# Another order of issue, and other engines for some copies, in the second feed-forward of an attention kernel

## The chip, the core and the metric

The kernel runs on one core of a Trainium2 chip. TensorE (PE) multiplies matrices into PSUM, VectorE (DVE) and ScalarE (ACT) do the work between matmuls, and SyncE (SP) issues the DMA transfers. Each engine works through its own list of instructions in order and waits on semaphores for the others. PEld is PE's weight load, which the profile shows apart. The metric is the device time of the program in microseconds.

## The reference

Windowed attention with global tokens gives 2176 rows of 512 numbers for the feed-forwards, which follow one another:

```python
def reference(**kwargs):
    ...
    attn_out = _attn_ref(**attn_kwargs)
    B, H, S, D = attn_out.shape
    x = np.ascontiguousarray(attn_out.transpose(0, 2, 1, 3)).reshape(B * S, H * D)
    x = _moe_ref(x=x, **moe_kwargs)      # h = x @ w_in;  (h * tanh(softplus(h))) @ w_out
    return _moe2_ref(x=x, **moe2_kwargs)
...
def _moe2_ref(x, w_in, w_out) -> np.ndarray:
    h = x @ w_in
    g = h * np.cos(h)
    return (g @ w_out).astype(np.float32)
```

All is float32; x is 2176 x 512, w_in 512 x 2048, w_out 2048 x 512. The attention and the first feed-forward are the same in both kernels.

## The kernel before

**Products in three parts.** A float32 matmul is made of three passes of a narrower type: each operand is split into a high and a low part, and low x high, high x high and high x low are added in PSUM. The high part is a cast (`gh`), the low part the difference (`gl`).

**The second feed-forward** is the function `second` (L952). It works in 24 steps s = 0 to 23: two halves p of the hidden units, three pairs of token blocks b (two of 384 tokens each, the last pair of 320 each), four groups of units j. Steps 0 to 11 are p = 0, steps 12 to 23 p = 1; steps 8 to 11 and 20 to 23 are the 320-wide pair. One step has these parts, which a list names by a letter, a number and the step:

- `P0` to `P6` (L1019): the first matrix product. A 2 x 2 block product is made of seven products in place of eight; the combined blocks of x are the operands 0 to 6. Each is six matmuls into one of two PSUM banks that they take in turns.
- `E0` to `E7` (L1041): the sums of those seven into the hidden values `hs`. `E0` is a copy of the product into `u`, the others are additions on DVE. A bank is free for the next product only when its sum or sums are done.
- `f0` to `f6`, `g0` to `g6` (in the last step `a`, `b`, `c`, `d`): h cos h for the two halves of the units. ACT does the first pair of operations (L831, L832) and a later pair (L841, L842), DVE L835, L838, L845; number 5 is the cast into `gh`, number 6 the difference `gl` on DVE (L851).
- `U0` to `U5`, `V0` to `V5` (L1050): units of the second product, three matmuls of 512 columns each, on accumulators 0 to 5 (one for each 128 tokens), U for the first half of the hidden units of a step and V for the second. They add up over the four steps j of a pair.
- `Z0` to `Z5`: an accumulator is emptied after step j = 3: copied into `part` (p = 0) or added to it on DVE and stored to the output (p = 1, L1068).
- `X`, `Y`: the weights of U or V are used up, and SP loads those of the next half into their place (L430, `w<-scr`). `A`, `I`, `L`: the operands of the next pair are formed, cast and stored to memory (L919, L345 or L347, L932, L940); after each product of a step j = 3 SP loads the operand of the next pair (L950 for `xo`, L947 for `xq`).
- `R`, `S`: what is left of the first feed-forward, in step 0.

**Tiles of PSUM.** Accumulators 0 and 1 are single banks (`acc_...`). Accumulators 2 and 3 are the halves of one tile, 4 and 5 of another (both named `h_...`). The program's dependencies go by tile: a unit on one half waits for a copy that reads the other half, and a copy of one half waits for a unit on the other.

**What sets the order.** A list written out by hand, the string `ORDER2` (L68), has some 1,079 entries such as `P0:11` or `Z5:7d`. It is run from its start to its end (L1080), and each entry issues its instructions on the engines that they belong to, DMAs included; so it sets the order on every engine at once. A last letter chooses the engine of a copy or cast (`move`, L341): d is DVE (L345), a is ACT (L347).

```python
        for step in ORDER2.split():
            name, _, n = step.partition(":")
            at2["at"] = n[-1:]
            steps[name](int(n.rstrip("ad")))
```

Which half of which tile an accumulator is, and which bank a product takes, stands in these lines:

```python
                single = [late["ps"].tile([P, 512], F32, tag="acc", name="acc", bufs=4) for _ in range(4)]
                acc.extend(single[2:4] + [t[:, c] for t in (ps2, ps) for c in range(2)] + single[0:2])
...
            i = (s + o) % 2
...
            return singles()[6 + i][:, 0:n_of(s)]
```

Of the kernel before, what the change touches and what calls it, by code (L numbers as in the profile page):

```python
# [65 lines left out]
"""  # L66

ORDER2 = """  # L68
    I6:0d L5:0 I0:1a P0:0 P1:0 E0:0d L6:0 P2:0 R:0 E1:0 I4:1a E2:0 L4:1 P3:0 P4:0 A5:1 E3:0 L0:1 E4:0 A3:1 f0:0
# [4 lines left out]
    P0:3 f0:2 P1:3 f1:2 V5:0 g5:1a E0:3a E1:3 U0:1 A6:1 P2:3 U4:1 f2:2 g6:1 f3:2 P3:3 I6:1d g0:2 U1:1 V1:1 E2:3
    f4:2 P4:3 L6:1 E3:3 E4:3 g1:2 U2:1 g2:2 U3:1 L4:2 U5:1 P5:3 P6:3 V3:1 f5:2a E6:3 g3:2 V0:1 f0:3 E7:3 A5:2 E5:3
    V2:1 P0:4 P1:4 g4:2 g5:2a E0:4a f6:2 V5:1 f1:3 A3:2 U2:2 E1:4 f2:3 P2:4 P3:4 E2:4 U5:2 P4:4 V4:1 U4:2 U0:2 f3:3
    g0:3 I0:2a g6:2 g1:3 E3:4 E4:4 g2:3 U1:2 f4:3 f0:4 g3:3 U3:2 f5:3a P6:4 P5:4 E6:4 E5:4 V5:2 L0:2 E7:4 V0:2 P0:5
    V4:2 E0:5a g4:3 f6:3 P1:5 g5:3a V3:2 f1:4 E1:5 I1:2d P2:5 P3:5 V1:2 U4:3 f2:4 V2:2 E2:5 I3:2a f3:4 E3:5 P5:5
    P4:5 g6:3 L1:2 L3:2 U0:3 V0:3 f4:4 g0:4 I5:2a U2:3 g1:4 U3:3 g2:4 A2:2 V4:3 V2:3 E4:5 P6:5 g3:4 E5:5 E6:5 E7:5
    g4:4 P0:6 P1:6 U1:3 Z4:3d f0:5 E0:6d U5:3 V1:3 f5:4a E1:6 f6:4 f1:5 A6:2 I2:2d Z0:3a f2:5 g5:4a P2:6 P3:6 E2:6  # L80
    f3:5 E3:6 V3:3 Z1:3a U0:4 V5:3 U4:4 P5:6 L5:2 g6:4 P4:6 f4:5 g0:5 V0:4 Z3:3d g1:5 U1:4 U3:4 E6:6 Z5:3a E4:6
    V3:4 E5:6 g2:5 f5:5a I6:2a L6:2 Z2:3a U5:4 P6:6 f0:6 f6:5 V1:4 E7:6 P0:7 U2:4 f1:6 P1:7 E0:7d g3:5 g4:5 L2:2
    P2:7 E1:7 V2:4 f2:6 V4:4 g5:5d E2:7 g0:6 U3:5 f3:6 P3:7 g6:5 P4:7 E3:7 E4:7 g1:6 f4:6 V5:4 g2:6 f5:6d f6:6 U1:5
    U4:5 f0:7 P5:7 g3:6 E6:7 P6:7 f1:7 U0:5 U2:5 E5:7 f2:7 V1:5 f3:7 E7:7 g4:6 V2:5 V0:5 P0:8 U5:5 P1:8 g5:6d E0:8a
    P2:8 f4:7 U0:6 V4:5 E1:8 E2:8 g6:6 P4:8 P3:8 g0:7 g1:7 V3:5 U4:6 E3:8 E4:8 P5:8 V5:5 U1:6 U2:6 g2:7 U5:6 E5:8
    E6:8 P6:8 P0:9 f0:8 g3:7 E7:8 f5:7d f6:7 U3:6 V5:6 f1:8 P1:9 E0:9d f2:8 g4:7 V1:6 V4:6 P2:9 g0:8 U1:7 E1:9
    g5:7d V3:6 g6:7 U4:7 g1:8 E2:9 f3:8 P3:9 P4:9 f4:8 U3:7 E3:9 P5:9 g2:8 V0:6 V2:6 U0:7 E5:9 E4:9 P6:9 f5:8d V3:7
    g3:8 f0:9 E6:9 E7:9 g4:8 U5:7 P0:10 P1:10 U2:7 f6:8 Z3:7a V1:7 E0:10d V2:7 P2:10 g5:8a E1:10 f1:9 f2:9 Z1:7d
# [5 lines left out]
    f4:11 g3:11 P6:12 P5:12 U0:10 E6:12 E5:12 f5:11d f0:12 U3:10 f6:11 E7:12 Z5:7d Y:8 P0:13 g4:11 V4:10 U2:10
    V2:10 f1:12 f2:12 E0:13a P1:13 g0:12 P2:13 E1:13 g5:11d P3:13 E2:13 g6:11 V1:10 P4:13 g1:12 V3:10 U1:11 X:8
    E3:13 E4:13 f3:12 V0:10 P5:13 P6:13 U2:11 g2:12 f4:12 E5:13 E6:13 g3:12 E7:13 P0:14 E0:14a P1:14 g4:12 E1:14
    f5:12a V2:11 f0:13 f6:12 P2:14 P3:14 U4:11 V4:11 V1:11 Z4:11a f1:13 U3:11 U0:11 E2:14 Z1:11a V3:11 Y:9 P4:14
    Z2:11a f2:13 U4:12 E3:14 E4:14 U5:12 P5:14 f3:13 g0:13 g5:12d V0:11 U1:12 U2:12 f4:13 g6:12 P6:14 g1:13 g2:13
    V5:12 E5:14 g3:13 E6:14 P0:15 E7:14 Z3:11d Z0:11d V2:12 U3:12 P1:15 E0:15d f5:13a f0:14 U0:12 X:9 g4:13 f6:13
    V0:12 f1:14 E1:15 P2:15 E2:15 V3:12 V1:12 f2:14 P3:15 g5:13d Y:10 E3:15 U5:13 P4:15 g6:13 g0:14 P5:15 g1:14  # L100
    U0:13 U1:13 E4:15 f3:14 f4:14 E6:15 g2:14 E5:15 U3:13 P6:15 E7:15 g3:14 g4:14 P0:16 U2:13 V2:13 V4:12 f5:14a
    P1:16 E0:16d P2:16 V1:13 U4:13 E1:16 V4:13 f0:15 X:10 g5:14a P3:16 X:11 f6:14 E2:16 f1:15 f2:15 P4:16 g0:15
    E3:16 f3:15 g6:14 P5:16 U4:14 V5:13 E4:16 V3:13 g1:15 U5:14 U3:14 g2:15 f0:16 P6:16 f4:15 g3:15 E6:16 E5:16
    P0:17 V0:13 E7:16 E0:17a U0:14 P2:17 f5:15a U1:14 g4:15 P1:17 f6:15 U2:14 V1:14 f1:16 E1:17 V5:14 E2:17 f2:16
    P4:17 Y:11 P3:17 V4:14 V0:14 V3:14 E3:17 g5:15d g6:15 f3:16 f4:16 E4:17 P5:17 g0:16 V2:14 Y:20 g1:16 P6:17
    E5:17 E6:17 U3:15 V3:15 g2:16 U1:15 E7:17 U4:15 P0:18 E0:18d P1:18 g3:16 g4:16 U0:15 f5:16d E1:18 P2:18 f0:17
    P3:18 f6:16 V1:15 U5:15 V5:15 U2:15 f1:17 E2:18 f2:17 f3:17 Z1:15 V4:15 E3:18 P5:18 f4:17 P4:18 g0:17 Z4:15
    Z3:15 Y:21 V2:15 U3:16 E4:18 Z5:15 g5:16a g6:16 V0:15 E5:18 E6:18 Z2:15 P6:18 U1:16 g1:17 V1:16 U4:16 U5:16
    g2:17 f5:17d f0:18 f6:17 V4:16 P0:19 V5:16 Z0:15 g3:17 E7:18 f1:18 g4:17 U2:16 U0:16 U5:17 g5:17d f2:18 E0:19a
    V3:16 P2:19 P1:19 U3:17 E1:19 f3:18 f4:18 E2:19 V0:16 P3:19 X:20 U4:17 E3:19 g0:18 g6:17 P4:19 V2:16 g1:18  # L110
    E4:19 P5:19 U2:17 g2:18 P6:19 E6:19 U1:17 E5:19 V4:17 f5:18a V5:17 E7:19 g3:18 P0:20 g4:18 f6:18 U0:17 E0:20d
    f0:19 g5:18d P1:20 f1:19 P2:20 E1:20 V0:17 f2:19 P3:20 E2:20 V2:17 f3:19 g6:18 U4:18 E3:20 P4:20 f4:19 P5:20
    E5:20 U5:18 E4:20 E6:20 V1:17 V5:18 V3:17 g0:19 P0:21 Y:22 P6:20 U2:18 g1:19 g2:19 U0:18 E7:20 f5:19d U3:18
# [1136 lines left out]
```

## Time and profile before

| what | us |
|---|---|
| median of three runs | 885.45 (883.87 to 886.25) |
| the profiled run | 883.55 |
| its span in the trace | 881.8 |
| PE busy in the span | 860.8 (98%) |
| DVE busy | 738.2 (84%) |
| ACT busy | 483.3 (55%) |

The mean granted clock of PE is 0.997 of full speed. The second feed-forward takes the time from 508.6 us to the end. In a timeline each row is one instruction or a run of equal ones, with its start, its length, how many they are (x6), and in brackets how long the engine had been idle before and what released it. Matmuls are pipelined, so a row's length reaches into the next row: the pace of PE is read from one start to the next.

### The profile page before, as it was taken

The numbers are of one execution on the slowest core, as the hardware profiler recorded it, in microseconds if no ns is written. First come the engines' busy times: TensorE is split into PE (matmuls) and PEld (weight loads), VectorE is DVE, ScalarE is ACT, GpSimd is POOL, SyncE is SP. The second block draws the span as 40 slices with busy tenths as digits, with TensorE's granted clock in tenths as the row PEclk, the third lists the DMA queues.
The fourth block names the chain that finished last, engine by engine and source line by source line (L and its number), as shares of the span: only waits on it lengthen the run. The fifth ranks groups of instructions, "written<-read, shape, count | busy, mean of one in ns | idle before, by whom it ended". The sixth has DMA issues, their size and how long they took to land.

```text
span 881.8 us, 16128 instructions
## 1 busy us (share of the span) xinstructions
PE 860.8 (98%) x5995; PEld 790.4 (90%) x5995; DVE 738.2 (84%) x1513; ACT 483.3 (55%) x948; POOL 85.9 (10%) x137
## 2 busy tenths in 40 slices
...
GB/s 161 198 158 161 168 152 74 49 156 215 233 252 266 328 338 361 286 294 237 277 243 193 387 414 220 283 90 148 234 144 321 109 14 355 1 79 202 1 60 72
DMA packets 133886, 174.98 MB, mean 198 GB/s; under 512 B 77872, under 2 KB 100400, under 8 KB 133808
## 3 DMA queue, kind: packets, MB, share of 16 engines
...
## 4 chain that ended last, share of the span: by engine, by line
PE 76%; DMA 10%; DVE 8%; ACT 3%; issue 2%; SPq 0%; POOL 0%; DVEq 0%; ACTq 0%; POOLq 0%
PE acc L1019 17%; PE acc L1118 14%; PE h L1050 13%; PE acc L1050 7%; PE h L795 5%; PE h L797 5%; PE h L796 5%; DMA cs<-in_moe_w_out_dram 4%; DMA cs<-in_moe_w_in_dram 2%; PE s L563 2%; PE av L633 1%; DVE ca L237 1%; DMA op<-stage 1%; PE ta L606 1%; DVE x L772 1%
## 5 line engine op out<-in xcount | busy, mean ns | idle before, releaser
L1118 PE MATMUL acc<-gh,w 128*128 128x384 f32 (+1 forms) x768 | 187.9, 328 | 0.0
L1118 PEld LDWEIGHTS acc<-gh,w 128*128 128x128 f32 x768 | 136.2, 189 | 0.0
L1118 PE MATMUL acc<-gl,w 128*128 128x384 f32 (+1 forms) x384 | 126.2, 329 | 2.9 <-DVE x L868 1.9
L795 PE MATMUL h<-x,w 128*128 128x384 f32 (+1 forms) x384 | 126.1, 328 | 0.6 <-DVE x L772 0.5
L797 PE MATMUL h<-x,w 128*128 128x384 f32 (+1 forms) x384 | 125.2, 326 | 0.0
L796 PE MATMUL h<-x,w 128*128 128x384 f32 (+1 forms) x384 | 125.1, 326 | 0.0
L1050 PE MATMUL h<-w,gh 128*128 128x512 f32 x352 | 109.8, 393 | 0.0
L1019 PE MATMUL acc<-xo,w 128*128 128x384 f32 (+1 forms) x402 | 76.4, 327 | 1.6 <-DVE hs L1041 1.6
L1050 PEld LDWEIGHTS h<-w,gh 128*128 128x128 f32 x352 | 66.1, 188 | 11.8
L1118 PEld LDWEIGHTS acc<-gl,w 128*128 128x128 f32 x384 | 72.6, 189 | 4.2 <-DVE x L868 2.2
L1019 PEld LDWEIGHTS acc<-xo,w 128*128 128x128 f32 x402 | 68.0, 188 | 6.6 <-DVE hs L1041 2.8
L841 ACT ACTIVATE w<-w 128x768 f32<-128x768 f32 (+2 forms) x50 | 39.0, 780 | 63.5 <-DVE w L838 63.5
L795 PEld LDWEIGHTS h<-x,w 128*128 128x128 f32 x384 | 72.1, 188 | 1.5 <-issue 0.8
L796 PEld LDWEIGHTS h<-x,w 128*128 128x128 f32 x384 | 72.1, 188 | 0.0
L797 PEld LDWEIGHTS h<-x,w 128*128 128x128 f32 x384 | 72.1, 188 | 0.0
L1050 PE MATMUL h<-w,gl 128*128 128x512 f32 x176 | 69.2, 393 | 2.2 <-DVE part L345 1.0
L1041 DVE TENSOR_TENSOR hs<-u,acc 128x384 f32<-128x384 f32 (+1 forms) x91 | 47.4, 526 | 28.3 <-PE acc L1019 26.9
L831 ACT ACTIVATE k<-hs,magic 128x768 f32<-128x768 f32 (+2 forms) x50 | 43.5, 871 | 49.2 <-DVE w L838 43.1
L1050 PE MATMUL acc<-w,gh 128*128 128x512 f32 x192 | 59.9, 393 | 0.0
L582 ACT ACTIVATE pr<-pr,nm 128x160 f32<-128x160 f32 x128 | 53.2, 421 | 10.6 <-DVE nm L579 10.4
L835 DVE SCALAR_TENSOR_TENSOR w<-k,hs 128x768 f32<-128x768 f32 (+2 forms) x50 | 44.0, 881 | 8.2 <-ACT k L832 6.5
L822 DVE TENSOR_TENSOR gl<-w,gh 128x768 fp32r<-128x768 f32 (+1 forms) x48 | 43.5, 907 | 8.3 <-ACT gh L818 8.3
...
## 6 DMA issues: line engine op xcount, KB each, us to landing
...
xo<-op SPq DMA_DIRECT2D x10, 640.0 KB, 4.9
```

Source lines behind the costliest of these rows:

```text
L582: nc.scalar.activation(out=pr[:, i], in_=pr[:, i], func=AF.Exp, bias=nm[:, i:i + 1], scale=-1.0, accum_out=l[:, i:i + 1])
L795: nc.tensor.matmul(ps[:, c, 0:n], wh[:, k, :], xl, start=(k == 0), stop=False)
L796: nc.tensor.matmul(ps[:, c, 0:n], wh[:, k, :], xh, start=False, stop=False)
L797: nc.tensor.matmul(ps[:, c, 0:n], wl[:, k, :], xh, start=False, stop=(k == NK - 1))
L822: nc.vector.tensor_tensor(out=gl, in0=v["w"], in1=gh.bitcast(F32), op=ALU.subtract)
L831: nc.scalar.activation(out=k[:, y], in_=of("h")[:, z], func=AF.Identity, scale=INV2PI, bias=magic[:, 0:1])
L835: nc.vector.scalar_tensor_tensor(out=of("t")[:, z], in0=k[:, y], scalar=-C1, in1=of("h")[:, z], op0=ALU.mult, op1=ALU.add)
L841: nc.scalar.activation(out=of("t")[:, z], in_=of("t")[:, z], func=AF.Sin, scale=0.5)
L1019: nc.tensor.matmul(to, l[:, i + c], r, start=c == 0 and m == 0, stop=c == 1 and m == 2)
L1041: nc.vector.tensor_tensor(out=of[out](), in0=of[x](), in1=bank(s, o), op=ALU.add)
L1050: nc.tensor.matmul(singles()[a], l[:, a * P:(a + 1) * P], r, start=(j, c) == (0, 0) and m == 0, stop=(j, c) == (3, 1) and m == 2)
L1118: nc.tensor.matmul(o[:, 0:n], w[:, a * P:(a + 1) * P], r[:, c, :], start=(not goes_on and g == 0 and m == 0), stop=(not stays and g == G - ...
```

## The change

Only the string `ORDER2` is another. It holds the same entries, but stands in another order from its first line to its last, and some copies and casts change engine: of the copies Z of p = 0 twelve are on ACT and not nine, of the E0 sixteen and not fourteen, of the operand casts I thirteen and not eleven, of the casts f5 and g5 twenty-five and not twenty-four. Instructions on PE and DMA transfers are the same in number and size. As text, around the end of step 11 (before, then after):

```diff
...
-    P6:11 U4:9 g3:10 g4:10 V4:9 f4:10 V2:8 f5:10a V1:9 f0:11 E5:11 E6:11 P0:12 E7:11 V0:9 f6:10 E0:12a P1:12 P2:12
+    V0:9 f6:10 g2:10 U2:9 P5:11 V2:9 E4:11 g3:10 E5:11 U4:9 g4:10 E6:11 V4:9 P6:11 g5:10d Z5:7d f0:11 P0:12 E7:11
...
```

Three places follow as the engines see them. A row names the line, the operation, what is written, what is read and the shape; numbers behind names tell buffers apart, and are not the same in the two kernels.

**First place: the end of step 10 and P0 of step 11.** `part` is the copy Z, `u` and `hs` the sums, `h_6599` the tile of accumulators 2 and 3, `acc_6762` and `acc_6763` the two banks of the products before, `acc_6768` and `acc_6769` after. DVE before:

```order
L835 SCALAR_TENSOR_TENSOR w_7888<-k_6598,hs_7770 128x640
L838 SCALAR_TENSOR_TENSOR w_7888<-k_6598,w_7888 128x640
L345 COPY part_7815<-h_6599 128x512
L1041 TENSOR_TENSOR u_6597<-u_6597,acc_6763 128x320
L1041 TENSOR_TENSOR hs_7896<-u_6597,acc_6763 128x320
L1041 TENSOR_TENSOR hs_7896<-u_6597,acc_6762 128x320
L345 COPY part_7815<-h_6596 128x512
```

Behind the copy of `h_6599` stand three sums. PE before, with P0:11 as the sixth row:

```order
L1050 MATMUL h_6599<-w1_0_6516,gh_7781 128x512 x2
L1019 MATMUL acc_6762<-xq_6600,w0_5_6481 128x320 x3
L1019 MATMUL acc_6762<-xq_6601,w0_5_6481 128x320 x3
L1050 MATMUL h_6599<-w1_1_6518,gl_7869 128x512
L1050 MATMUL h_6599<-w1_1_6518,gh_7831 128x512 x2
L1019 MATMUL acc_6763<-xo_6128,w0_6_6551 128x320 x6
```

The product on `acc_6763` stands directly behind the unit V3:8 on `h_6599`. DVE after:

```order
L835 SCALAR_TENSOR_TENSOR w_7874<-k_6598,hs_7772 128x640
L851 TENSOR_TENSOR gl_7897<-w_7807,gh_7876 128x640
L838 SCALAR_TENSOR_TENSOR w_7874<-k_6598,w_7874 128x640
L1041 TENSOR_TENSOR hs_7900<-u_6597,acc_6769 128x320
L1041 TENSOR_TENSOR u_6597<-u_6597,acc_6769 128x320
L1041 TENSOR_TENSOR hs_7900<-u_6597,acc_6768 128x320
L835 SCALAR_TENSOR_TENSOR w_7917<-k_6598,hs_7842 128x640
L345 COPY part_7837<-acc_6770 128x512
```

The sums have no copy of `h_6599` ahead of them; those copies are on ACT. PE after, with P0:11 as the last row:

```order
L1019 MATMUL acc_6769<-xq_6591,wt_6376 128x320 x3
L1019 MATMUL acc_6769<-xq_6592,wt_6376 128x320 x3
L1019 MATMUL acc_6768<-xq_6606,w0_5_6481 128x320 x3
L1019 MATMUL acc_6768<-xq_6607,w0_5_6481 128x320 x3
L1050 MATMUL acc_6771<-w1_0_6516,gl_7805 128x512
L1050 MATMUL acc_6771<-w1_0_6516,gh_7796 128x512 x2
L1050 MATMUL h_6599<-w1_0_6516,gl_7805 128x512
L1050 MATMUL h_6599<-w1_0_6516,gh_7796 128x512 x2
L1050 MATMUL h_6599<-w1_1_6518,gl_7849 128x512
L1050 MATMUL h_6599<-w1_1_6518,gh_7811 128x512 x2
L1050 MATMUL h_6599<-w1_2_6584,gl_7897 128x512
L1050 MATMUL h_6599<-w1_2_6584,gh_7876 128x512 x2
L1019 MATMUL acc_6769<-xo_6128,w0_6_6551 128x320 x6
```

Between the product on `acc_6769` (two rows at the top, P5:10) and the next one there are now a product and four units.

**Second place: Z5:7, the copy of accumulator 5 out of the tile `h_6596`, and the next unit on that tile.** DVE before:

```order
L1041 TENSOR_TENSOR u_6597<-u_6597,acc_6763 128x384
L1041 TENSOR_TENSOR hs_8130<-u_6597,acc_6763 128x384
L345 CAST gh_8132<-w_8065 128x640
L851 TENSOR_TENSOR gl_8139<-w_8065,gh_8132 128x640
L1041 TENSOR_TENSOR hs_8130<-u_6597,acc_6762 128x384
L345 COPY part_8142<-h_6596 128x512
L845 SCALAR_TENSOR_TENSOR w_8103<-w_8103,hs_8037 128x640
```

The copy is the sixth row. PE before:

```order
L1050 MATMUL h_6599<-w1_4_6745,gh_8030 128x512 x2
L1019 MATMUL acc_6763<-xo_6128,w0_2_7696 128x384 x6
L1050 MATMUL h_6596<-w1_5_6747,gl_8085 128x512
L1050 MATMUL h_6596<-w1_5_6747,gh_8083 128x512 x2
L1050 MATMUL h_6599<-w1_4_6745,gl_8050 128x512
```

The unit V4:10 on `h_6596` (w1_5) is on the other half of that tile. DVE after:

```order
L845 SCALAR_TENSOR_TENSOR w_7984<-w_7984,hs_7900 128x640
L1041 TENSOR_TENSOR u_6597<-u_6597,acc_6768 128x320
L345 CAST gh_8048<-w_7984 128x640
L345 COPY part_8050<-h_6596 128x512
L1041 TENSOR_TENSOR hs_8028<-u_6597,acc_6769 128x320
L835 SCALAR_TENSOR_TENSOR w_8061<-k_6598,hs_7966 128x640
L345 COPY u_6597<-acc_6768 128x384
```

The copy now stands ahead of the last sum of step 11 (`hs_8028`, E7:11). PE after, from the product that this sum reads (P6:11):

```order
L1019 MATMUL acc_6769<-xq_6606,w0_7_6553 128x320 x3
L1019 MATMUL acc_6769<-xq_6607,w0_7_6553 128x320 x3
L1019 MATMUL acc_6768<-xo_6128,w0_0_7596 128x384 x6
L1050 MATMUL acc_6771<-w1_3_6586,gl_7981 128x512
L1050 MATMUL acc_6771<-w1_3_6586,gh_7979 128x512 x2
L1019 MATMUL acc_6769<-xo_6128,w0_0_7596 128x384 x6
L1019 MATMUL acc_6768<-xo_6128,wb_6369 128x384 x6
L1050 MATMUL h_6599<-w1_3_6586,gl_7981 128x512
L1050 MATMUL h_6599<-w1_3_6586,gh_7979 128x512 x2
L1019 MATMUL acc_6769<-xo_6128,w0_1_7655 128x384 x6
L1019 MATMUL acc_6768<-xo_6128,wt_6368 128x384 x6
L1019 MATMUL acc_6769<-xq_6591,wt_6368 128x384 x3
L1019 MATMUL acc_6769<-xq_6592,wt_6368 128x384 x3
L1050 MATMUL h_6596<-w1_4_6738,gl_8007 128x512
```

The next unit on `h_6596` (U4:10) is the last row; none of the rows between writes that tile.

**Third place: SP's queue while steps 12 to 15 run.** `w0_` and `w1_` are weights, `xo` the operands. Before:

```order
L430 DMA w0_7_8015<-scr31_0_6221 128x1024
L430 DMA w1_1_8144<-scr25_1_5602 128x1024
L430 DMA w1_0_8210<-scr24_1_5467 128x1024
L430 DMA w1_3_8303<-scr27_1_5810 128x1024
L950 DMA xo_6128<-op1_0_6664 128x1536
L950 DMA xo_6128<-op1_1_6810 128x1536
L430 DMA w1_2_8393<-scr26_1_5703 128x1024
L950 DMA xo_6128<-op1_2_6876 128x1536
L950 DMA xo_6128<-op1_3_6827 128x1536
```

The load of w1_2 stands behind two operand loads. After:

```order
L430 DMA w0_7_8046<-scr31_0_6221 128x1024
L430 DMA w1_2_8112<-scr26_1_5703 128x1024
L430 DMA w1_1_8171<-scr25_1_5602 128x1024
L430 DMA w1_4_8220<-scr28_1_5945 128x1024
L430 DMA w1_3_8223<-scr27_1_5810 128x1024
L430 DMA w1_5_8271<-scr29_1_6059 128x1024
L950 DMA xo_6128<-op1_0_6699 128x1536
L950 DMA xo_6128<-op1_1_6869 128x1536
L430 DMA w1_6_8379<-scr30_1_6207 128x1024
L430 DMA w1_7_8388<-scr31_1_6297 128x1024
```

Five loads of w1 stand ahead of the first operand load.

## Rows read from the trace of the kernel before

**Rows 1.** Page, span and section 1: busy us (share), instructions, by engine.

```profile
span 881.8 us, 16128 instructions
...
PE 860.8 (98%) x5995; PEld 790.4 (90%) x5995; DVE 738.2 (84%) x1513; ACT 483.3 (55%) x948; POOL 85.9 (10%) x137
```

**Rows 2.** Waits of PEld, 508 to 882: us in total, times, longest us.

```profile
PEld acc L1019 <- DVE hs L1041: 4.0, 7, 2.0
PEld h L1050 <- DVE part L345: 1.6, 2, 1.3
```

**Rows 3.** Chain that ended last: start us, us, what; pieces without a wait.

```profile
734.56 2.10 PE acc L1019 x12
...
809.86 0.88 PE acc L1019 x6
...
813.88 0.69 PE h L1050 x3
```

**Rows 4.** Timeline of PE: start us, us, engine line op out<-in xcount [idle before <-releaser].

```profile
529.97 0.39 PE L1050 MATMUL h<-w,gl 128*128 128x512 f32 x1
...
531.33 0.96 PE L1019 MATMUL acc<-xq,w 128*128 128x384 f32 x4 [0.50 <-DVE hs L1041]
...
543.98 1.31 PE L1019 MATMUL acc<-xq,w 128*128 128x384 f32 x6
...
661.84 0.39 PE L1050 MATMUL h<-w,gl 128*128 128x512 f32 x1
...
664.27 2.02 PE L1019 MATMUL acc<-xo,w 128*128 128x320 f32 x12 [1.57 <-DVE hs L1041]
...
693.31 1.23 PE L1019 MATMUL acc<-xo,w 128*128 128x384 f32 x6
695.52 0.50 PE L1050 MATMUL h<-w,gl 128*128 128x512 f32 x1 [0.98 <-DVE part L345]
...
725.10 0.50 PE L1050 MATMUL h<-w,gl 128*128 128x512 f32 x1
...
731.48 1.21 PE L1019 MATMUL acc<-xo,w 128*128 128x384 f32 x6
733.60 0.50 PE L1050 MATMUL h<-w,gl 128*128 128x512 f32 x1 [0.92 <-DMA w<-scr]
...
781.11 1.21 PE L1019 MATMUL acc<-xo,wt 128*128 128x384 f32 x6
782.58 0.50 PE L1050 MATMUL h<-w,gl 128*128 128x512 f32 x1 [0.27 <-DVE part L1068]
```

**Rows 5.** Timeline of DVE around the first two stalls.

```profile
662.74 0.69 DVE L345 COPY part<-h 128x512 f32<-128x512 f32 x1 [1.93 <-PE h L1050]
663.34 0.48 DVE L1041 TENSOR_TENSOR u<-u,acc 128x320 f32<-128x320 f32 x1
663.74 0.88 DVE L1041 TENSOR_TENSOR hs<-u,acc 128x320 f32<-128x320 f32 x2
...
694.78 0.68 DVE L345 COPY part<-h 128x512 f32<-128x512 f32 x1
```

**Rows 6.** Timeline of SP's queue ahead of the third stall.

```profile
725.19 2.98 SPq L950 DMA_DIRECT2D xo<-op  x2
728.22 0.42 SPq L430 DMA_DIRECT2D w<-scr  x1
```

**Rows 7.** Waits of SP, 600 to 640, then 640 to 760: total, times, longest.

```profile
SPq L950 <- DMA op<-stage: 7.3, 1, 7.3
...
SPq L950 <- PE acc L1019: 51.5, 10, 35.5
```

**Rows 8.** One tile, op (stored operands), 600 to 635: us from issue to landing.

```profile
DMA to landing us min/median/max: 2.9/6.5/8.4
```

**Rows 9.** DMA issues: out<-in, engine, op, times, KB, median us to landing.

```profile
op<-stage SPq DMA_DIRECT2D x7, 640.0 KB, 3.0
```

**Rows 10.** Waits of ACT, 508 to 882: total, times, longest.

```profile
ACT stage L347 <- DMA op<-stage: 7.3, 5, 3.8
```

More of the change, by code (lines that the diff above doesn't have):

```diff
@@ L74 @@
[L74 to L88, printed above, removed]
@@ L94 @@
[L94 to L108, printed above, removed]
@@ L109 @@
[L109 to L113, printed above, removed]
@@ new lines @@
+    V0:0 P5:2 f4:1 I5:1a P6:2 f0:2 f5:1a E6:2 L5:1 I2:1a U4:0 U3:0 E5:2 E7:2 V4:0 V3:0 g3:1 L2:1 P0:3 V5:0 f6:1
+    g4:1 E0:3a f1:2 V1:0 A6:1 P1:3 g5:1a I6:1a P2:3 U0:1 E1:3 U2:1 P3:3 f2:2 E2:3 g0:2 g6:1 g1:2 f3:2 P4:3 U4:1
+    V4:1 E3:3 I4:2a P5:3 g2:2 U3:1 E4:3 g3:2 U5:1 V3:1 f4:2 L6:1 f5:2a E6:3 f6:2 P6:3 f0:3 E5:3 g4:2 E7:3 f1:3 V5:1
+    L4:2 V0:1 U0:2 U1:1 f2:3 P0:4 E0:4d P1:4 E1:4 P2:4 g5:2d V2:1 g0:3 E2:4 P3:4 V1:1 g6:2 P4:4 f3:3 f4:3 f5:3a
+    U3:2 A5:2 g1:3 E3:4 U2:2 g2:3 V3:2 E4:4 P5:4 E5:4 E6:4 f0:4 P6:4 U4:2 g3:3 U5:2 P0:5 f6:3 A3:2 E7:4 I0:2d I3:2a
@@ new lines @@
+    f1:4 V5:2 g4:3 U3:3 P1:5 E0:5a U1:2 f2:4 f3:4 E1:5 V1:2 L0:2 P2:5 P3:5 g5:3a V0:2 L3:2 I1:2a E2:5 V2:2 E3:5
+    P4:5 P5:5 f4:4 g6:3 U2:3 U1:3 E4:5 g0:4 g1:4 U5:3 V4:2 V2:3 E5:5 E6:5 I5:2a g2:4 P6:5 L1:2 U4:3 f5:4a A2:2 g3:4
+    P0:6 f6:4 E7:5 L5:2 V1:3 E0:6a U0:3 g4:4 f0:5 A6:2 Z1:3a P1:6 g5:4d E1:6 f1:5 P2:6 P3:6 V3:3 f2:5 I6:2a V4:3
+    Z2:3a f3:5 Z3:3a E2:6 Z4:3a E3:6 P4:6 E4:6 P5:6 P6:6 E6:6 V5:3 f4:5 V0:3 g0:5 g6:4 U4:4 E7:6 I2:2a U3:4 Z5:3a
+    Z0:3a g1:5 L2:2 f5:5d V3:4 U5:4 U0:4 E5:6 P0:7 U2:4 g2:5 V4:4 g3:5 g4:5 P1:7 E0:7a V2:4 f6:5 E1:7 U1:4 f0:6
@@ new lines @@
+    P3:14 E2:14 E3:14 U3:11 P4:14 E4:14 P5:14 P6:14 g5:12d E5:14 Z1:11a E6:14 V3:11 E7:14 P0:15 g0:13 Z2:11d f5:13a
+    U0:12 g6:12 Z3:11a U3:12 P1:15 U1:12 E0:15a X:11 f6:13 U2:12 g1:13 Y:11 Z4:11a g2:13 g3:13 U4:12 V4:12 g4:13
+    V2:12 g5:13d f0:14 E1:15 f1:14 f2:14 V3:12 P2:15 P3:15 E2:15 V0:12 U0:13 f3:14 U2:13 V5:12 Y:20 U4:13 g6:13
+    E3:15 g0:14 g1:14 V1:12 f4:14 P4:15 U1:13 E4:15 P5:15 g2:14 f5:14d E6:15 f6:14 U3:13 P6:15 E5:15 V1:13 f0:15
+    P0:16 V0:13 U5:13 f1:15 f2:15 E7:15 V3:13 V4:13 P1:16 g3:14 V2:13 X:20 E0:16a U4:14 f3:15 Y:21 f4:15 P2:16
@@ new lines @@
+    V5:13 g4:14 g5:14d E1:16 P3:16 g0:15 Y:22 U5:14 U3:14 g6:14 V3:14 E2:16 P4:16 g1:15 E3:16 g2:15 f5:15d g3:15
+    P5:16 U2:14 E4:16 V2:14 g4:15 Y:23 P6:16 V5:14 f6:15 U0:14 f0:16 E6:16 E5:16 E7:16 U1:14 f1:16 P0:17 E0:17d
+    P1:17 g5:15a E1:17 P2:17 f2:16 P3:17 V1:14 f3:16 E2:17 E3:17 g0:16 V4:14 g6:15 P5:17 P4:17 V0:14 U1:15 f4:16
+    E6:17 f5:16a g1:16 g2:16 U5:15 U2:15 U3:15 E4:17 P6:17 E5:17 E7:17 V3:15 g3:16 f0:17 P0:18 P1:18 f6:16 U0:15
+    V0:15 f1:17 U4:15 E0:18a f2:17 g4:16 g5:16a V5:15 E1:18 P3:18 g6:16 Z0:15 Z5:15 P2:18 V1:15 E2:18 E3:18 g0:17
@@ new lines @@
+    g1:17 U5:16 f3:17 P4:18 P5:18 V5:16 Z3:15 g2:17 E4:18 X:21 f4:17 V4:15 Z1:15 g3:17 V2:15 E6:18 P6:18 U0:16
+    f5:17a U1:16 f0:18 E5:18 P0:19 Z2:15 f6:17 E7:18 g4:17 P1:19 Z4:15 E0:19d E1:19 f1:18 f2:18 V0:16 U2:16 P2:19
+    P3:19 g0:18 U4:16 U3:16 V4:16 E2:19 U0:17 g5:17a P4:19 V1:16 E3:19 U4:17 f3:18 g6:17 V0:17 V3:16 V2:16 E4:19
+    g1:18 P5:19 f4:18 g2:18 f5:18d E5:19 E6:19 P6:19 V4:17 U5:17 f0:19 g3:18 f6:18 X:22 U1:17 g4:18 E7:19 f1:19
+    P0:20 P1:20 E0:20d U2:17 P2:20 U3:17 f2:19 E1:20 P3:20 E2:20 U4:18 P4:20 E3:20 V5:17 g5:18d E4:20 f3:19 f4:19
@@ new lines @@
+    V2:17 P5:20 g6:18 g0:19 V1:17 U2:18 P6:20 V4:18 V3:17 U5:18 U3:18 g1:19 E5:20 E6:20 E7:20 P0:21 U1:18 g2:19
+    f5:19a P1:21 g3:19 f6:19 U0:18 V3:18 f0:20 g4:19 E0:21a f1:20 E1:21 P2:21 P3:21 V5:18 V2:18 f2:20 U2:19 E2:21
+    g5:19d g6:19 E3:21 P4:21 f3:20 f4:20 P5:21 U3:19 g0:20 E5:21 V1:18 E6:21 g1:20 E4:21 g2:20 P0:22 V0:18 U4:19
+    g3:20 V3:19 U0:19 X:23 V0:19 f5:20a P6:21 f6:20 Z3:19 U5:19 U1:19 f0:21 E7:21 E0:22d Z0:19 f1:21 g4:20 P1:22
+    P2:22 E1:22 V1:19 V5:19 f2:21 Z1:19 V2:19 E2:22 V4:19 g5:20a P3:22 g0:21 Z2:19 g6:20 U0:20 Z4:19 P4:22 E3:22
```

45 lines of the change are left out of this document (25 added, 20 removed).

## The prediction, made before the result was known

> **What bounds the kernel now.** I read five views in this order. First the page: a span of 881.8 us in a profiled run of 883.55, with PE busy 98% and DVE 84% [rows 1]. So PE sets the time, and a change of order can give back only what PE waits for. The run shown is 1.9 us under the median of the three (885.45); I sum against the run and carry the saving to the median one for one. A difference of 0.3%, 2.66 us, is about what a measurement of this kernel can tell from none.
>
> Second, where PE waits: the diff touches ORDER2 alone, so nothing before 508 us moves. After it the largest entry is PE's weight loads waiting for the sums on DVE, 4.0 us in 7 times; then copies of part on DVE, 1.6 us in 2 [rows 2]. Third, PE's rows from start to start. Three pieces give its pace without waits: six 384-wide matmuls 1.05 us, six 320-wide 0.88, a unit of three 512-wide 0.69 [rows 3]. A row that starts later than the row ahead plus its pace is a stall [rows 4]:
> at 664.27, due 661.84 + 0.69 = 662.53: 1.74;
> at 695.52, due 693.31 + 1.05 = 694.36: 1.16;
> at 733.60, due 731.48 + 1.05 = 732.53: 1.07;
> at 531.33, due 529.97 + 0.69 = 530.66: 0.67;
> at 782.58, due 781.11 + 1.05 = 782.16: 0.42.
> That makes 5.06. The matmul behind a stall is late once more by about 0.1 (the first one takes 0.50 at 733.60 where 0.39 is usual at 661.84), five times 0.5: **5.6 us in five places**. Five smaller ones of 0.1 to 0.2 each, the first at 543.98 and the last at 725.10 [rows 4], make 0.7, and with the matmul behind each 1.2. All of it is **6.8 us**; the rest of PE's time in this stretch is work, which the change leaves as it is.
>
> Fourth, who was late, on DVE and on the SP queue. At 664.27 the product waits for two sums that start at 663.34 and 663.74; they stood behind a copy of one half of a PSUM tile, which had DVE idle 1.93 us until 662.74, because a unit on the other half of the same tile (661.84) had to end first [rows 4, 5]. At 695.52 the unit waits for a copy of the other half, started at 694.78 as the last of a full queue. At 733.60 it waits for a weight load that SP issued at 728.22, after two operand loads had gone from 725.19 [rows 6]; these loads wait in SP for products, once for 35.5 us [rows 7], and SP keeps its order. The other two are a sum and an addition on DVE that came late.
>
> **The change, part by part.** It is the same list of steps in another order, with some copies and casts given to the other engine. The PE and DMA instructions are the same in number and shape, so every part is priced by what it makes wait.
>
> (a) *First place (P0:11).* Now a product and four units lie between the end of P5:10, whose sums free the bank, and P0:11: 0.88 + 4 x 0.69 = 3.64 us of PE. DVE needs 0.2 (the step from PE), two sums of 0.48 [rows 5] that overlap by 0.08, and 0.05 back: 1.1. That leaves 2.5 us for rows queued ahead. The copy of that tile (Z3:7) is now on ACT, with rows of a gate behind it and no sum. It is still tied, to U2:8; the unit that needs it, U3:8, comes after two products and a unit, 2 x 0.88 + 0.69 = 2.45 us later, and a copy needs 0.2 + 0.69 + 0.05 = 0.94. So 1.74 + 0.1 goes. If ACT comes late there by more than the 1.5 that are left, the rest of its delay comes back.
>
> (b) *Second place (Z5:7 and units on its tile).* The copy now stands ahead of E7:11 on DVE. The bank of that sum must be free before P1:12, and from there PE has five products and a unit, 5 x 1.05 + 0.69 = 5.9 us, before U4:10, the next unit on the tied tile. So the copy cannot be what PE waits for: 1.16 + 0.1 goes.
>
> (c) *Third place (SP).* The load of w1_2 moves ahead of all loads of the next pair's operands, and so do w1_4 and w1_5. It needed 733.60 - 728.22 = 5.4 us from issue to use, the 0.05 step in it. Counting PE's work between the instruction that frees a buffer and the first one that reads it again, with SP's order in between, the smallest such room for w1_2's kind of load was 4.85 us before and is 9.9 over all loads after; the slowest of the loads read took 8.4 [rows 8]. The operand loads now have more refills ahead of them, but their own rooms are in that 9.9. So 1.07 + 0.1 goes, with 1.5 us of cover left.
>
> The Trainium skill (DMA: Bandwidth & Descriptors, section Anatomy of one DMA) prices a transfer at 2.0 us plus its bytes at 436 GB/s, 3.2 us for these 512 KB, an estimate from that page; by it the load would have landed at 731.4 and the stall would not be there, so (c) would bring nothing and the saving would be 1.2 less. The trace disagrees, since PE starts at the landing, 5.4 us after the issue, and the sum goes by the trace.
>
> (d) *The two others* (531.33 and 782.58) are DVE rows that came late by less than one row. I walked the order of after by the same durations (sums 0.48 and, 384 wide, 0.55; copies 0.68; 0.2 and 0.05 for the steps between engines). Before, 7 of PE's waits on one engine alone come out short, by 1.72, 1.24, 1.12, 0.77 and less, at places that match the stalls above; after, none does, and the tightest has 0.15 us. Taking these two as gone brings 0.67 + 0.42 + 0.2 = 1.3.
>
> (e) *What is paid.* Twenty-eight of 215 waits have under 0.5 us of room after. A duration varies by about 0.1, so small stalls stay. I take the five of before, 1.2 us, as they are. The bounds: none of them, 0, if all rooms hold; 3.4 if each of the 17 places with 0.3 or less is late by 0.1 and pays the 0.1 behind it. I choose 1.2 because it is what this very stage shows in such places now. Three more copies of part, two first sums, two operand casts and one gate's cast go from DVE to ACT, which is busy 55% of the time against DVE's 84 [rows 1]; 0 is taken for it, with (a) and the second rival as the places where it could cost.
>
> The sum: 5.6 saved of 6.8, with 1.2 staying. The run of 883.55 becomes 877.95 (span 876.2), the median 885.45 - 5.6 = **879.9**. The ends of the sum alone: 885.45 - 6.8 = 878.6, and 885.45 - 6.8 + 3.4 = 882.0.
>
> **The rivals.** *A wait takes its place: the late store.* In after's order operand 6 of the third pair is made and stored late (L6:2), then loaded for P6:8. PE has 12.2 us of work between the end of that subtraction and P6:8. SP waited 7.3 us for one such store [rows 7], and a load may take 8.4 [rows 8]; 7.3 + 8.4 = 15.7, which is 3.5 too much. So 879.9 + 3.5 = **883.4**, within 0.3%. For it: the worst of both has been seen in this stage. Against it: a store of this size lands in 3.0 at the median [rows 9], and with 8.4 that makes 11.4, under 12.2.
>
> *Slower: ACT waits for stores.* A cast of an operand on ACT must wait until the store from the same buffer has landed. Five such waits took 7.3 us in all, 1.5 each, and PE lost nothing by them [rows 10]. After's order has three with little room: by the durations of the rows between, 1.25, 2.99 and 3.16 us from the issue of the store to the cast's turn. With 3.0 the first waits 1.75 and the others about nothing. If each store took 7.3, ACT would stand 6.05 + 4.31 + 4.14 = 14.5 us in these three places, and with 1.5 of cover each 10.0 would reach PE: 879.9 + 10.0 = **889.9**. It turns to slower by over 0.3% when what reaches PE is over 8.3, a cover under 2.1 us. Against it: of the stores in this stage one took that long, not three.
>
> *The change does not do what it says.* The stalls could come back at places that my walk rates as tight by luck of the durations: all 28 places under 0.5 late by the 0.1 and paying the 0.1 behind would give 5.6 back: **885.5**, no difference. For it: the walk is blind to what a loaded memory does to rows. Against it: before, the same walk puts the five large stalls where they are.
>
> **How the numbers follow.** The forecast (five stalls gone, small ones stay) 0.72; small stalls up to twice as many, to 882.5, still faster by over 0.3%: 0.08; late store 0.08; no difference 0.05; slower 0.07. So faster 0.80, same 0.13, slower 0.07. The range goes from 877.0 (the 878.6 of the sum, less the 1.6 by which the lowest of the three runs lies under their median) to 884.0, which takes in the late store; what is left out is the end of the two last cases.
>
> **What would show it.** In after's trace: PE's waits on sums fall from 4.0 us to under 1; no gap of PE over 0.4 us after 510; the DVE copies of part release no matmul; no weight load releases a unit. From the first product to the last unit PE needs 5 to 6 us less than now. It is wrong if PE shows one wait over 1 us on a load of operand 6 or on a gate's row behind an operand cast of ACT, or if more than ten small stalls stand where I count five.

## The result, and the profile after

The changed kernel took 876.16 us, median of five runs (874.99 to 878.04), against 885.33 of five of the kernel before: a ratio of 0.9904 with an interval of 0.9886 to 0.9921. The medians are 9.2 us apart; ratio and interval come from the single runs and not from the two medians (whose ratio is 0.9896), and put the saving at 8.5 us, 7.0 to 10.1. A saving of 5.6 had been forecast, and 876.16 lies below the range, whose end was 877.0. The profiled run took 874.99 us, with a span of 873.2.

The page after, span and busy time by engine (answers to [rows 1]):

```profile
span 873.2 us, 16132 instructions
...
PE 857.3 (98%) x5995; PEld 790.1 (90%) x5995; DVE 733.1 (84%) x1506; ACT 486.9 (56%) x955; POOL 85.9 (10%) x137
```

The first view to read is again where PE's weight loads wait, now from 508 to 875 (answers to [rows 2]; us in total, times, longest). There is one row and no other:

```profile
PEld acc L1019 <- DVE hs L1041: 0.5, 1, 0.5
```

Next PE's rows (start, length, instruction), at the start of the second feed-forward, around P0:11, around U4:10, at the one stall that is left, and at the end (answers to [rows 4]):

```profile
507.05 2.27 PE L1019 MATMUL h<-xo,w 128*128 128x384 f32 x12
...
660.48 0.39 PE L1050 MATMUL h<-w,gl 128*128 128x512 f32 x1
...
661.16 1.92 PE L1019 MATMUL acc<-xo,w 128*128 128x320 f32 x12
...
682.89 1.20 PE L1019 MATMUL acc<-xq,wt 128*128 128x384 f32 x6
683.93 0.39 PE L1050 MATMUL h<-w,gl 128*128 128x512 f32 x1
...
732.78 0.39 PE L1050 MATMUL acc<-w,gl 128*128 128x512 f32 x1
...
733.65 1.32 PE L1019 MATMUL acc<-xo,w 128*128 128x384 f32 x6
...
868.60 0.61 PE L1050 MATMUL h<-w,gh 128*128 128x512 f32 x2
```

P0:11 starts at 661.16, where 660.48 + 0.69 = 661.17 was due; before it was 1.74 late. U4:10 starts at 683.93, due 682.89 + 1.05 = 683.94; before, the unit at this place was 1.16 late. The row at 733.65 is 0.18 late (732.78 + 0.69 = 733.47) and the matmul behind it by 0.1: 0.3 us is all that is left of 6.8. In the kernel before, the same two ends of the stretch are

```profile
508.58 2.27 PE L1019 MATMUL h<-xo,w 128*128 128x384 f32 x12
...
877.16 0.61 PE L1050 MATMUL h<-w,gh 128*128 128x512 f32 x2
```

The second matmul of such a pair starts 0.23 after the first, so from the first product to the last matmul's start it was 877.39 - 508.58 = 368.8 us and is 868.83 - 507.05 = 361.8. The second feed-forward, then, gave **7.0 us**. Of the 8.6 us between the two profiled spans the other 1.5 lie ahead of the first product (508.58 and 507.05), where both kernels issue the same instructions in the same order.

SP's queue has the third place (answers to [rows 6]): six weight loads went out in a row, the last of them 20 us ahead of the operand loads, and no weight load releases PE any more.

```profile
677.22 18.41 SPq L430 DMA_DIRECT2D w<-scr  x6
715.61 2.75 SPq L950 DMA_DIRECT2D xo<-op  x2
```

ACT's waits for stores, 505 to 875 (answers to [rows 10]), fell from 7.3 us in five to 2.2 in two:

```profile
ACT stage L347 <- DMA op<-stage: 2.2, 2, 1.8
```

### The profile page after: what moved, and what is told of

Read it like the earlier page. It is cut to its first block, busy times and chain, and to the rows that moved or that the text cites. A ratio compares the mean times of both kernels' runs of the same rounds, so it can differ in the third digit from the quotient of the medians.

```text
span 873.2 us, 16132 instructions
## 1 busy us (share of the span) xinstructions
PE 857.3 (98%) x5995; PEld 790.1 (90%) x5995; DVE 733.1 (84%) x1506; ACT 486.9 (56%) x955; POOL 85.9 (10%) x137
## 4 chain that ended last, share of the span: by engine, by line
PE 79%; DVE 9%; DMA 8%; ACT 2%; issue 1%; SPq 0%; POOL 0%; DVEq 0%; ACTq 0%; POOLq 0%
PE acc L1019 18%; PE acc L1118 15%; PE h L1050 14%; PE acc L1050 8%; PE h L795 5%; PE h L796 5%; PE h L797 5%; DMA cs<-in_moe_w_out_dram 4%; DMA cs<-in_moe_w_in_dram 2%; PE s L563 2%; DVE ca L237 2%; PE ta L606 1%; PE av L633 1%; ACT pr L582 1%; PE h L1019 1%
## 5 line engine op out<-in xcount | busy, mean ns | idle before, releaser
L845 DVE SCALAR_TENSOR_TENSOR w<-w,hs 128x768 f32<-128x768 f32 (+2 forms) x50 | 43.9, 879 | 14.0 <-ACT w L842 13.7
L851 DVE TENSOR_TENSOR gl<-w,gh 128x768 fp32r<-128x768 f32 (+2 forms) x50 | 43.8, 878 | 9.4 <-ACT gh L347 9.1
```

Source lines behind the costliest of these rows:

```text
L845: nc.vector.scalar_tensor_tensor(out=of("t")[:, z], in0=of("t")[:, z], scalar=1.0, in1=of("h")[:, z], op0=ALU.subtract, op1=ALU.mult, reve ...
L851: nc.vector.tensor_tensor(out=of("gl")[:, z], in0=of("t")[:, z], in1=of("gh")[:, z].bitcast(F32), op=ALU.subtract)
```

## The experiments

**The two kernels again.** No edit. Each was run and profiled twice more.

> The kernel before, unchanged, in another execution. Two readings of the 8.6 us between the two profiled runs (7.0 from the first product to the last unit, 1.5 ahead of it). Order theory: what PE loses in the second feed-forward is set by the order, so the five large stalls come back at the same places with the same sizes (1.7, 1.2, 0.7, 0.4 within 0.1; the one behind a weight load, 1.1, within 0.5) and the small ones too; first product to last unit 369.0 within 0.5; the 1.5 us ahead of the first product is chance and falls out otherwise here. Rival, chance: small stalls at other places, the stretch off by more than 1. The time is the same as before's, a ratio of 1.000 within 0.002.

> The kernel before once more, for a third look at the stretch from the first product to the last unit: 368.8 us in both executions so far. Store theory: the stall after 531 is ACT's wait for the store less 0.46 us, so it is 0.7 to 2 here and the stretch 368.7 to 370; the others repeat to 0.02, but for the weight load (0.7 to 1.7). Rival: the two executions are typical, 368.8 again within 0.1.

> The changed kernel, unchanged, in another execution. Order theory: under 0.5 us of stalls after the first product again, 362.0 us from there to the last unit, and a ratio that is 7.0 us plus chance, 0.992. Rival: the first execution was a lucky one, small stalls of 1 us or more in all turn up, and the ratio goes to 0.993 or more. A second rival: something beyond the second feed-forward gained too, then the ratio is 0.990 or less.

> The changed kernel once more: 361.8 us in both executions so far. Store theory: 361.8 within 0.1 again, since nothing in this order waits for a transfer; one stall of 0.16 to 0.18 and the 0.1 behind it. Rival: more than 0.5 us of stalls.

The times: 886.64 against 885.59 of the same kernel (ratio 1.000, 0.9977 to 1.0022), and 877.44 for the changed one (0.990, 0.9871 to 0.9928); the third executions took 888.95 and 873.48, one run each. The ratio of the changed one, 0.990, is where the second rival put it (something beyond the second feed-forward gained too), but its interval takes in the 0.992 of the order theory, so it decides nothing. From the first product to the last matmul the kernel before needs 368.8, 368.8 and 369.6 us, the changed one 361.8 in all three. The stalls of before come back at the same places: at P0:11 1.74 three times; at V4:10 1.16, 1.16 and 1.17; the addition 0.43 three times; the weight load 1.07, 0.81 and 1.09; of the five small ones four come back to 0.01, and the first is 0.16, 0.15 and 0.08. They are set by the order. One is not: the stall after 531 was 0.67, 0.90 and 1.37. What differs there is one row on ACT, a cast of an operand that waits for a store (start, length, in brackets the wait), here of before, of before again, of before for the third time, and of the run with other ties below:

```profile
526.18 0.83 ACT L347 CAST stage<-x 128x768 fp32r<-128x768 f32 x1 [1.13 <-DMA op<-stage]
```

```profile
527.83 0.83 ACT L347 CAST stage<-x 128x768 fp32r<-128x768 f32 x1 [1.35 <-DMA op<-stage]
```

```profile
531.55 0.83 ACT L347 CAST stage<-x 128x768 fp32r<-128x768 f32 x1 [1.82 <-DMA op<-stage]
```

```profile
531.07 0.83 ACT L347 CAST stage<-x 128x768 fp32r<-128x768 f32 x1 [2.53 <-DMA op<-stage]
```

PE's stalls were 0.67, 0.90, 1.37 and 2.07: each is ACT's wait less 0.45 or 0.46. The chain runs from the store over the cast I3:1 to the two ACT rows of g0:0 that stand behind it, to L835 and L838 on DVE, to a sum, to PE. DVE's part of it in the kernel before, ahead of PE's row at 531.33:

```profile
528.86 0.96 DVE L835 SCALAR_TENSOR_TENSOR w<-k,hs 128x768 f32<-128x768 f32 x1 [0.66 <-ACT k L832]
529.85 0.96 DVE L838 SCALAR_TENSOR_TENSOR w<-k,w 128x768 f32<-128x768 f32 x1
530.73 0.55 DVE L1041 TENSOR_TENSOR hs<-u,acc 128x384 f32<-128x384 f32 x1
```

This order lets the landing of a store through to PE, one for one, and the changed one does not. That explains 0 to 0.8 us by which before can be longer than in its first profile. What it does not explain is the time ahead of the first product, 508.6, 510.0 and 513.2 us before and 507.1, 511.8 and 505.5 after: within one kernel it varies by 4.7 and 6.3 us, nearly as much as the whole effect.

**Five moves in the old order.** The stalls one by one, each by moving the step that was waited for:

```diff
-    ... P5:1 g2:0 E4:1 L1:1 ...
+    ... P5:1 E4:1 g2:0 L1:1 ...
-    ... V3:8 Z2:7d E6:10 E5:10 E7:10 Z0:7a ...
+    ... V3:8 E6:10 E5:10 E7:10 Z2:7d Z0:7a ...
-    ... E2:12 P3:12 ... E7:12 Z5:7d Y:8 ...
+    ... E2:12 Z5:7d P3:12 ... E7:12 Y:8 ...
-    ... E6:14 P0:15 ... U0:12 X:9 g4:13 ...
+    ... E6:14 X:9 P0:15 ... U0:12 g4:13 ...
-    ... P5:18 f4:17 P4:18 g0:17 Z4:15 Z3:15 Y:21 ...
+    ... P5:18 Z3:15 f4:17 P4:18 g0:17 Z4:15 Y:21 ...
```

> The kernel before with five entries of its list moved and nothing else: the two copies of part, one addition, one sum and one weight load that the five large stalls waited for. Order theory (each stall is its own): all five go, the small ones stay at 1 to 1.5 us; 363.4 us from first product to last unit, ratio 0.9937 (5.6 us). Rival (only a whole new order can do it, since each move makes something else late): two or more of the five come back elsewhere, 366 us or more, ratio 0.996 or more.

880.91 us, ratio 0.9937 (0.9911 to 0.9963), 364.8 us in the stretch where 363.4 had been expected. Four of the five stalls are gone, at both copies, at the weight load and at the addition, and nothing came in their place. The one after 531 became two, 0.60 and 0.82. PE's rows of this kernel:

```profile
533.65 0.39 PE L1050 MATMUL h<-w,gl 128*128 128x512 f32 x1
...
534.95 1.32 PE L1019 MATMUL acc<-xq,w 128*128 128x384 f32 x6 [0.43 <-DVE hs L1041]
...
537.61 1.32 PE L1019 MATMUL acc<-xo,w 128*128 128x384 f32 x6 [0.65 <-DVE u L1041]
```

The sum was moved ahead of g2:0 (L838) and still came late, since it stood behind g1:0 (L835), which waited for ACT; L838 and a subtraction now stood ahead of the next sums and made those late. ACT's cast waited 2.05 us for its store in this run. DVE's row ahead of the sum that was moved:

```profile
533.47 0.96 DVE L835 SCALAR_TENSOR_TENSOR w<-k,hs 128x768 f32<-128x768 f32 x1 [1.58 <-ACT k L832]
```

**Five moves, the first one another.** As above, but E4:1 stays and the cast goes behind the gate:

```diff
-    ... E0:1a f6:0 I3:1a R:3 S:3 g0:0
+    ... E0:1a f6:0 R:3 S:3 g0:0 I3:1a
```

> The kernel before with five entries moved, as in the run with five moves, but for the stall after 531 it is now a cast of ACT (I3:1) that goes behind two rows of a gate (g0:0) and no longer a sum. Store theory (that stall comes from a store on which the cast waits, with the gate's rows behind it): the stall and the one that the wrong move brought are gone, small ones of 1.2 us stay, 362.9 to 363.4 us from first product to last unit, ratio 0.9925 to 0.993. Rival (DVE's own queue is late there): a stall of 0.6 or more stays.

880.81 us, ratio 0.9949 (0.9928 to 0.9969), 364.3 us in the stretch. No stall is left at 531. But PE, earlier by that, runs into the next cast that waits for a store, with a first sum (E0:2, `u<-acc`) behind it on ACT. ACT's and PE's rows:

```profile
538.42 0.83 ACT L347 CAST stage<-x 128x768 fp32r<-128x768 f32 x1 [1.82 <-DMA op<-stage]
539.16 0.47 ACT L347 COPY u<-acc 128x384 f32<-128x384 f32 x1
```

```profile
537.97 0.63 PE L1050 MATMUL acc<-w,gh 128*128 128x512 f32 x2
539.68 0.98 PE L1019 MATMUL acc<-xo,wb 128*128 128x384 f32 x4 [1.08 <-ACT u L347]
```

That costs 1.25 + 0.1, and the 362.9 to 363.4 us expected were missed by 1. **The same move alone** (one run, as for each edit below but for the other ties):

> The kernel before with that one cast moved behind g0:0 and nothing else. Store theory: ACT still waits 1 to 2.5 us for the store, but with nothing urgent behind it, so the stall after 531 falls under 0.2; the other four and the small ones stay as they were (1.74, 1.15, 0.8 to 1.7, 0.43). Rival, DVE's queue: 0.6 to 2 us stay.

The stretch took 368.0 us. The stall after 531 is gone, the next one is 0.56 at 541; the other four stand where they stood, 1.74, 1.15, 0.76 and 0.44. So the expectation held for its stall and missed what is behind it: several casts wait for stores one after the other, and a single move pushes the wait to the next cast.

**The same cast put back in the new order.**

```diff
-    ... R:2 R:3 E0:1a f5:0a g1:0 ... g4:0 I3:1a P5:1 ...
+    ... R:2 R:3 E0:1a I3:1a f5:0a g1:0 ... g4:0 P5:1 ...
```

> The changed kernel with the same cast (I3:1) put ahead, directly behind E0:1 on ACT, as it stood in the kernel before. Store theory: ACT waits about 3 us there (the store is issued at 514.9 and takes about 10, the cast's turn comes at 521.9), the gate's cast behind it comes late, and PE loses 1 to 3 us within the next 15 us. Rival (the new order has cover for any of this): under 0.3 us.

ACT's rows, then PE's:

```profile
525.54 0.46 ACT L347 COPY u<-h 128x384 f32<-128x384 f32 x1
529.73 0.83 ACT L347 CAST stage<-x 128x768 fp32r<-128x768 f32 x1 [3.73 <-DVE u L1041]
530.47 0.83 ACT L347 CAST gh<-w 128x768 fp32r<-128x768 f32 x1
```

```profile
532.34 0.50 PE L1050 MATMUL acc<-w,gl 128*128 128x512 f32 x1 [1.41 <-DVE gl L851]
```

ACT stands 3.7 us, and PE loses 1.57 + 0.1; the stretch takes 363.5 us and not 361.8. The row names a sum on DVE as what ended ACT's wait, but that had ended at 529.44, and the cast reads nothing of it. The view of the stored tile, from 512 to 530, has how long its stores took:

```profile
DMA to landing us min/median/max: 7.0/8.7/10.3
```

The first was issued at 519.07, and 10.3 later is 529.4. That it was this store is an inference from these rows, and the 0.3 us from there to the cast's start stay open. One cast at another place, then, is worth 1.7 us in an order that is otherwise the new one.

**Stores made longer.** In both orders each of the seven stores of the second pair's operands goes out twice, the second time to a place that nobody reads:

```diff
                     nc.sync.dma_start(out=d.rearrange("p a c n -> p (a c n)"), in_=whole.bitcast(F32))
+                    if b == 1:
+                        d2 = dram.tile([P, 2, 2, n], F32, name=f"twice{o}")
+                        nc.sync.dma_start(out=d2.rearrange("p a c n -> p (a c n)"), in_=whole.bitcast(F32))
```

> The kernel before, but each of the seven stores of the second pair's operands is issued twice, the second time to a place that nobody reads, so that its buffer is free later. Store theory: ACT's waits for stores grow from 7 us to 12 or more, and PE loses 2 to 10 us more between 525 and 610 than without (368.8 becomes 371 to 379). Rival (stores are covered, as the prediction had it): under 1 us more.

> The changed kernel with the same seven stores issued twice. Store theory: the new order has more room at those casts (2.2 us of waits and no loss of PE), so it loses less than the kernel before does under the same stores, by at least 2 us; 361.8 becomes 362 to 368. Rival: both orders lose the same.

The stretch took 375.9 us in the old order and 364.7 in the new, so 6.3 to 7.1 more than without and 2.9 more. About 1.5 of the old order's loss is the granted clock, which fell behind its second stall (last section); without that the two losses differ by 1.9 to 2.7, with it by 3.4 to 4.2. ACT's waits for stores in the old order, expected at 12 us or more, are 11.0 in the row of the view for them; another of 3.8 is put down there to a sum, at a cast that waits for a store in the kernel before. In the old order the cast ahead of g0:0 waited 3.66, and PE 3.21 (the 0.45 again); then the next cast cost 3.19 more:

```profile
529.70 0.83 ACT L347 CAST stage<-x 128x768 fp32r<-128x768 f32 x1 [3.66 <-DMA twice<-stage]
...
542.20 0.83 ACT L347 CAST stage<-x 128x768 fp32r<-128x768 f32 x1 [3.79 <-DMA twice<-stage]
```

```profile
534.84 0.62 PE L1022 MATMUL acc<-xq,w 128*128 128x384 f32 x2 [3.04 <-DVE hs L1044]
...
543.46 1.92 PE L1022 MATMUL acc<-xo,wb 128*128 128x384 f32 x6 [3.02 <-ACT u L347]
```

In the new order ACT waited 3.35 at one cast as well, but PE lost 1.1 in the 14 us behind it, in three pieces of which the largest is 0.40. Another 1.05 and 0.43 of its loss are operand loads that came late: SP held them back until a store of the operand had landed, 9.6 us here and 7.2 in the changed kernel without the second stores:

```profile
539.25 0.84 ACT L347 CAST stage<-x 128x768 fp32r<-128x768 f32 x1 [3.35 <-DMA twice<-stage]
```

```profile
570.44 0.76 PE L1022 MATMUL acc<-xq,w 128*128 128x384 f32 x3 [0.26 <-DMA xq<-op]
572.08 0.79 PE L1022 MATMUL acc<-xq,w 128*128 128x384 f32 x3 [0.89 <-DMA xq<-op]
```

**Other ties.** The old order with its list as it is; only the accumulators that share a tile are others, 2 with 4 and 3 with 5:

```diff
-                acc.extend(single[2:4] + [t[:, c] for t in (ps2, ps) for c in range(2)] + single[0:2])
+                acc.extend(single[2:4] + [t[:, c] for c in range(2) for t in (ps2, ps)] + single[0:2])
```

> The kernel before with its order as it is, but accumulators 2 and 4 share a tile, and 3 and 5, in place of 2 with 3 and 4 with 5. Tie theory: the stalls at 664 and 695 came from the tie of halves, so both go (3.1 us with the matmul behind each), and the one at 783 (0.5) too, since the copy that a unit waits for is now another; what the new pairs tie elsewhere comes on top, unknown, 0 to 2 us. Ratio 0.996 to 0.999. Rival, queue on DVE alone: copies and sums are as late as before, both stalls stay at over 1 us.

882.39 us, ratio 0.9961 (0.9943 to 0.998), 367.7 us in the stretch. Both stalls at the copies are gone. At P0:11 DVE's copy starts at once behind the gate's row, with no wait for V3:8, and the sums behind it are in time (DVE's rows, then PE's):

```profile
665.54 0.82 DVE L838 SCALAR_TENSOR_TENSOR w<-k,w 128x640 f32<-128x640 f32 x1
666.29 0.68 DVE L345 COPY part<-h 128x512 f32<-128x512 f32 x1
666.89 0.48 DVE L1041 TENSOR_TENSOR u<-u,acc 128x320 f32<-128x320 f32 x1
```

```profile
667.40 0.39 PE L1050 MATMUL h<-w,gl 128*128 128x512 f32 x1
...
668.10 1.92 PE L1019 MATMUL acc<-xo,w 128*128 128x320 f32 x12
```

The same copy stands ahead of the same sums, so it was the tie and not DVE's queue that made them late. The new pairs brought a stall of 0.85 at another place (ACT's copy of a half, ahead of a unit on the other), and one addition costs 0.21; the rest of what is missing is that the store and the weight load came later in this run, with stalls of 2.07 and 1.66.

**One copy put back in the new order.** Z5:7 ahead of V4:10, as before:

```diff
-    ... g5:10d Z5:7d f0:11 ... E6:12 V4:10 ...
+    ... g5:10d f0:11 ... E6:12 Z5:7d V4:10 ...
```

> The changed kernel with one copy (Z5:7) put back to where the kernel before had it, directly ahead of V4:10 on its own tile. By the rows of the changed kernel the copy would start at 684.92 (in its times), end 0.68 later, and V4:10 was due at 685.32: a stall of 0.3 and the 0.1 behind it, 0.4 in all; nothing else over 0.2. Tie theory: this. Rival (copies near a unit cost nothing as long as DVE is not full): under 0.1.

DVE's copy, then PE's unit:

```profile
684.50 0.68 DVE L345 COPY part<-h 128x512 f32<-128x512 f32 x1
```

```profile
684.21 0.39 PE L1050 MATMUL h<-w,gl 128*128 128x512 f32 x1
...
685.24 0.50 PE L1050 MATMUL h<-w,gl 128*128 128x512 f32 x1 [0.18 <-DVE part L345]
```

685.24 - (684.21 + 0.69) = 0.34, and 0.1 behind it: 0.45 where 0.4 was expected. The stretch is 362.3, 0.5 longer than without. This stall could be worked out from the rows to a tenth.

## Why the prediction was right in sign and wrong in size

**Right: the direction, and four of the five large stalls.** (a), (b), (c) and the addition at 782.58 went, 4.8 us with the matmuls behind them, by the mechanisms named: a copy tied to the other half, a copy that came last, a load behind operand loads, an addition behind another. The five moves show that these four are separate, and the other ties that the first two were ties. None of the five moves changes an engine; what the other engines for some copies give by themselves was not run. No wait took the place of the four.

**Wrong: step (e), the small stalls.** This is the term of the sum that was mis-sized: 1.2 us went in, and 0.3 was measured. It let 1.2 us stay, because rows were held to vary by about 0.1 and 28 waits had under 0.5 of room. They do not vary by that in this stretch: four of the five small stalls come back to 0.01. After, 0.3 is left, at one place, 0.16 to 0.18 in each of three executions. With 0.3 for 1.2 the same sum gives 885.45 - 6.5 = 879.0. The end of the sum with no stall at all was 878.6, so this term alone does not bring it to 876.16.

**Wrong: (d), the cause of the stall at 531, and with it the second rival.** (d) called it a sum late by less than a row; the sum was late because ACT stood behind a store. The "ACT waits for stores" rival had the right mechanism with the wrong sign: it said of five such waits that PE lost nothing by them, while the first of them was the stall of 0.67, and it feared for the new order what the old one suffered. Its three tight places (1.25, 2.99 and 3.16) cost PE nothing; with the stores doubled the new order lost 2.9 and the old one over 6 (1.5 of it by the clock). The view that misled was the list of waits by the last releaser: PE's row names a sum on DVE, and only going back from there, sum to L838, to L835, whose idle time ends with `k L832`, to the cast and its store, shows where the time came from.

**The rest: the median, and the low end of the range.** The sum was 6.8; the stretch gave 7.0 (7.8 by the third execution of before), the first median moved by 9.2. Of the 3.6 us between this and the forecast of 5.6, then, 0.9 is (e), and 0.5 is time in the stretch that the sum does not list (at 537.04, 561.78 and 724.12 PE was late by 0.07 to 0.10, for instance). The other 2.2 go against two assumptions of the prediction: that nothing ahead of 508 us moves, and that the saving carries from one run to the median one for one. What they come from stays open, and the interval of the ratio, 7.0 to 10.1 us, takes in a saving that is the stretch alone. The range left 1.6 us below the sum for the scatter of a median, and one run scatters by more: of the kernel before, twelve runs lie between 882.16 and 888.95. The profiled run shown (883.55) was faster than all five timed ones, and in it ACT waited the least for the store. Whether something ahead of the first product gained too stays open. It starts at 505.5 to 511.8 us in six executions of the new order and its variants, 508.1 on average, and at 508.6 to 513.3 in eight of the old and its variants, 511.3; the ranges overlap, the instructions ahead are the same and in the same order, and no run here tells chance from a cause. Much of this scatter goes with the granted clock (last section).

**The other rivals.** The late store of operand 6 was covered: SP's rows show the store at 616.61 and the loads of the last two operands ending their issue at 622.1, where PE's P6:8 starts at 628.71 without a wait. That the stalls would come back elsewhere did not happen in the new order. In the old one it did: the cast that was moved let a wait through at the next cast (0.56 alone, 1.25 with the other four moves), the sum that was moved split its stall in two (0.60 and 0.82), and the other ties brought one of 0.85.

```profile
616.61 0.32 SPq L940 DMA_DIRECT2D op<-stage  x1
617.03 5.05 SPq L947 DMA_DIRECT2D xq<-op  x4
```

**The price of a transfer.** The section of the Trainium skill from which the prediction takes 3.2 us beside (c) (DMA: Bandwidth & Descriptors, Anatomy of one DMA) is on transfers that GpSimd issues, and the load here was issued by SP behind two others. So its 5.4 us say nothing against that price where it was taken; the sum rightly went by the trace.
